# The last product of a linear-attention and MLP kernel, by seven block products in place of eight

## The chip, the cores and the metric

The kernel runs on one core of a Trainium2 chip. The metric is the device time of one execution in microseconds (us), the median of several runs. The engines named below are TensorE (PE, with its weight loads as PEld), VectorE (DVE), ScalarE (ACT) and SyncE (SP), whose queue issues all DMAs here.

## The reference, cut to what matters

```python
kv  = einsum('bhsd,bhse->bhde', k, v)          # 8 batches, 8 heads, 576 tokens, 64 dims
o   = einsum('bhsd,bhde->bhse', q, kv)
x   = o / sqrt(mean(o*o) + 1e-6) * g_norm      # rows of heads joined: 4608 tokens x 512
h   = x @ w_in                                 # 512 x 2048
x   = (h * clip(h + 3, 0, 6) / 6) @ w_out      # 2048 x 512
g   = x @ w_gate; val = x @ w_val              # 512 x 1536 each
out = (g * sigmoid(g) * val) @ w_out2          # 1536 x 512: the last product
```

All of it is fp32; the weights arrive as 64-bit floats and are decoded on the chip.

## The kernel before, in words

A product of two fp32 matrices is made of three matmuls of rounded operands: each operand is split into a high part (ScalarE copies it into a rounded type) and a low part (VectorE subtracts the high part from the source), by `split`, L105; `mm3`, L110, multiplies high by low, low by high and high by high into one accumulator.

The second MLP has two stages. The gate/value stage (`gv_step`, L682; `quad`, L657) runs over six blocks of 768 tokens, each visited twice (`visits`, L935): once for the first half of the gate/value weights, then, in reverse order, for the second half. A visit has three steps, a step two quads, one of gate and one of value. A quad makes a two by two block of the result by seven products of sums (`product`, L647, six matmuls of 384 columns each) in place of eight; the sums of weights come from `combine`, L490, which makes seven operand tiles from two decoded weight tiles, and `operands`, L479, which names them; the sums of x come from `prepare_x`, L608. The seven tiles of most pairs of the second half are stored in DRAM (`wsd`) in the first visits and loaded back when the visits turn round (`reload`, L940). The result of a step, `hv`, goes to DRAM as `g2d` (L687), feature blocks of 128 by all tokens. 36 steps in all, `c` from 0 to 35; the second half of the visits is c = 18 to 35.

The last product (L986 to L996) multiplies `g2d` by w_out2. It runs over nine blocks of 512 tokens, from the last to the first, and in each over the twelve feature blocks f. `load_g2`, L692, loads 512 tokens of one f (256 KB) and splits them; `o2_step`, L701, takes the four slices of 128 tokens as stationary operands and the 512 columns of w_out2 as moving ones: 4 x 3 matmuls of 512 columns, each with a weight load. Loads are issued eight f ahead. After f = 11 the four accumulators are copied out and stored (L711 to L718). w_out2 is decoded and split in steps 18 to 21 (f = 0 to 3) and 33 to 35 (the other eight), L979 to L981.

Space: the pool `w` (L86) has 58 slots of 256 KB. 42 of them hold gate/value sums through the second half of the visits; the rest are for what is on its way. The PSUM pool `ps` (L929) has four tags of one bank each, twice.

The order of the work: TensorE's instructions run in the order in which they are written (`manual_schedule`, L723). For the other engines and for the DMA queue a planner orders the instructions at build time, by the order of the text and by what it reckons to be ready. Each engine and SP's queue then go through that order one by one.

## Time and profile before

| | |
|---|---|
| median of 3 runs | 1720.38 us (1719.48 to 1722.3) |
| the profiled execution | 1719.0 us from its first to its last instruction; no other time of it is given |
| TensorE busy | 1688.9 us, 98% of the span |
| VectorE busy | 1185.0 us, 69% |
| ScalarE busy | 773.3 us, 45% |
| DMA | 252 MB, 147 GB/s on average |
| gate/value stage | about 890 to 1419.5 us of the span |
| last product | 1419.6 to 1715.2 us |

TensorE is almost always busy, so the table says little by itself; what a stage costs is the number of its matmuls and the distance between their starts, and where that distance breaks, a wait stands behind it. A matmul's recorded length overlaps the next one's, so lengths are not to be summed; starts are to be compared. The distances and waits are in the rows further down.

### The profile page before, as it was taken

The numbers are of one execution on the slowest core, as the hardware profiler recorded it, in microseconds if no ns is written. First come the engines' busy times: TensorE is split into PE (matmuls) and PEld (weight loads), VectorE is DVE, ScalarE is ACT, GpSimd is POOL, SyncE is SP. The second block draws the span as 40 slices with busy tenths as digits, with TensorE's granted clock in tenths as the row PEclk, the third lists the DMA queues.
The fourth block names the chain that finished last, engine by engine and source line by source line (L and its number), as shares of the span: only waits on it lengthen the run. The fifth ranks groups of instructions, "written<-read, shape, count | busy, mean of one in ns | idle before, by whom it ended". The sixth has DMA issues, their size and how long they took to land.

```text
span 1719.0 us, 25593 instructions
## 1 busy us (share of the span) xinstructions
PE 1688.9 (98%) x9636; PEld 1493.1 (87%) x9636; DVE 1185.0 (69%) x2353; ACT 773.3 (45%) x1439; POOL 2.4 (0%) x7
## 2 busy tenths in 40 slices
PE   7999999999999999999999999999999999999999
PEld 3566789898898899998889999999999997888887
DVE  5897987778777777777889888777666685322321
ACT  4565554445444454545555444434443453222221
POOL 0000000000000000000000000000000000000000
PEclk8999999999999999999999999999999999999999
DMA  7886444454545444325465544572222235334332
GB/s 191 248 259 188 130 138 128 146 149 115 160 127 159 126 148 131 123 99 184 151 205 178 198 147 149 184 260 76 81 91 92 92 135 182 125 111 143 140 110 74
DMA packets 200171, 252.29 MB, mean 147 GB/s; under 512 B 79984, under 2 KB 129136, under 8 KB 200048
## 3 DMA queue, kind: packets, MB, share of 16 engines
q1 hardware_dynamic: 200048, 250.67, 45.0%
q8 instruction: 75, 1.23, 0.3%
q14 instruction: 48, 0.39, 0.1%
HBM read 185.86 MB, written 64.75 MB: 146 GB/s over the span
## 4 chain that ended last, share of the span: by engine, by line
PE 86%; DVE 8%; ACT 2%; DMA 2%; issue 1%; SPq 0%; DVEq 0%; ACTq 0%
PE q_g L651 14%; PE q_v L651 14%; PE acc L111 12%; PE acc L112 12%; PE acc L113 12%; PE a L651 6%; PE d L651 4%; PE c L651 4%; PE h L117 3%; PE kv L250 1%; DMA raw_g<-in_moe_w_gate_dram 1%; DVE lT L108 1%; DVE g L108 1%; DVE t L580 1%; PE at L112 0%
## 5 line engine op out<-in xcount | busy, mean ns | idle before, releaser
L111 PE MATMUL acc<-g,wo 128*128 128x512 f32 x512 | 202.1, 395 | 0.0
L112 PE MATMUL acc<-g,wo 128*128 128x512 f32 x512 | 199.9, 390 | 0.0
L113 PE MATMUL acc<-g,wo 128*128 128x512 f32 x512 | 199.5, 390 | 0.0
L108 DVE TENSOR_TENSOR g2l<-g,g2h 128x512 fp32r<-128x512 f32 x108 | 73.4, 692 | 139.1 <-ACT g2h L107 138.5
L111 PE MATMUL acc<-wl,g2h 128*128 128x512 f32 x432 | 168.2, 389 | 1.0 <-ACT g2h L107 1.0
L112 PE MATMUL acc<-wh,g2l 128*128 128x512 f32 x432 | 168.2, 389 | 0.3 <-DVE g2l L108 0.3
L113 PE MATMUL acc<-wh,g2h 128*128 128x512 f32 x432 | 168.1, 389 | 0.0
L579 ACT ACTIVATE t<-h,three 128x512 f32<-128x512 f32 x120 | 86.7, 722 | 138.8 <-DVE h L574 109.5
L107 ACT ACTIVATE g2h<-g 128x512 fp32r<-128x512 f32 x108 | 67.9, 632 | 147.7 <-PE acc L112 74.3
L107 ACT ACTIVATE g<-t 128x512 fp32r<-128x512 f32 x144 | 90.9, 631 | 88.8 <-DVE t L580 73.6
L108 DVE TENSOR_TENSOR g<-t,g 128x512 fp32r<-128x512 f32 x144 | 97.9, 680 | 31.6 <-ACT g L107 31.2
L113 PEld LDWEIGHTS acc<-g,wo 128*128 128x128 f32 x512 | 96.1, 188 | 20.5
L111 PEld LDWEIGHTS acc<-g,wo 128*128 128x128 f32 x512 | 96.2, 188 | 19.9
L112 PEld LDWEIGHTS acc<-g,wo 128*128 128x128 f32 x512 | 96.2, 188 | 18.3
L111 PEld LDWEIGHTS acc<-wl,g2h 128*128 128x128 f32 x432 | 81.1, 188 | 18.0 <-ACT g2h L107 1.4
L112 PEld LDWEIGHTS acc<-wh,g2l 128*128 128x128 f32 x432 | 81.1, 188 | 17.5 <-DVE g2l L108 0.6
L580 DVE SCALAR_TENSOR_TENSOR t<-t,h 128x512 f32<-128x512 f32 x120 | 82.6, 688 | 19.3 <-ACT t L579 15.7
L113 PEld LDWEIGHTS acc<-wh,g2h 128*128 128x128 f32 x432 | 81.1, 188 | 16.9
L117 PE MATMUL h<-x,w_i 128*128 128x512 f32 x192 | 87.0, 602 | 1.9 <-DVE w_i L170 1.9
L117 PEld LDWEIGHTS h<-x,w_i 128*128 128x128 f32 x192 | 36.7, 193 | 43.2 <-issue 40.2
L651 PE MATMUL q_v<-hT,v 128*128 128x384 f32 x288 | 73.6, 336 | 0.0
L679 ACT ACTIVATE hg<-q_g 128x384 f32<-128x384 f32 x36 | 17.6, 490 | 113.3 <-PE q_g L651 113.3
(245 smaller groups left out, 4483.3 us busy)
## 6 DMA issues: line engine op xcount, KB each, us to landing
wo<-wod SPq DMA_DIRECT2D x128, 512.0 KB, 3.4
g2d<-hv SPq DMA_DIRECT2D x36, 768.0 KB, 3.4
g<-g2d SPq DMA_DIRECT2D x108, 256.0 KB, 4.6
xr<-x1d SPq DMA_DIRECT2D x11, 1536.0 KB, 6.7
x1d<-x1o SPq DMA_DIRECT2D x36, 256.0 KB, 2.9
out_dram<-o SPq DMA_DIRECT2D x36, 256.0 KB, 2.1
raw_i<-in_moe_w_in_dram SPq DMA_DIRECT2D x16, 512.0 KB, 5.3
raw_o<-in_moe_w_out_dram SPq DMA_DIRECT2D x16, 512.0 KB, 4.4
```

The source lines that it names most:

```text
L107: nc.scalar.activation(out=hi, in_=src, func=AF.Copy)
L108: nc.vector.tensor_tensor(out=lo, in0=src, in1=f32(hi), op=ALU.subtract)
L111: nc.tensor.matmul(out_, wh, xl, start=start, stop=False)
L112: nc.tensor.matmul(out_, wl, xh, start=False, stop=False)
L113: nc.tensor.matmul(out_, wh, xh, start=False, stop=stop)
L117: nc.tensor.matmul(out_, f32(w), f32(x), start=start, stop=stop)
L250: nc.tensor.matmul(ps[h * D:(h + 1) * D, :D], kt[:, h, r, :], vt[:, h, r, :], start=i == 0, stop=i == len(steps) - 1,)
L579: nc.scalar.activation(out=t, in_=h[i], func=AF.Relu, bias=three[:, 0:1])
L580: nc.vector.scalar_tensor_tensor(out=t, in0=t, scalar=6.0, in1=h[i], op0=ALU.min, op1=ALU.mult)
L651: nc.tensor.matmul(ps, a[:, kk], b[:, kk], start=first and n == 0, stop=n == 5, skip_group_check=True,)
L679: nc.scalar.activation(out=h[:, 0], in_=a, func=AF.Copy)
```

## The change

The last product takes the form that the gate/value stage has. A pair q of feature blocks (2q and 2q+1) and two halves of 256 tokens make a two by two block of g; w_out2's two feature blocks and its two halves of 256 columns make one of the weights. Seven products of sums replace eight, and each is a row of matmuls of 256 columns.

It runs in two phases per block of tokens: first, over all six pairs, the four products that need T1, T3, B11 and T2 (`o2_one`), then, over all six pairs, the three that need B22, T4 and B21 (`o2_two`). Between the two, u and v are formed from the accumulators, and phase two adds to three of them. The operands of g are made for two pairs at once (a unit): `g_one` loads four feature blocks (1 MB) into one tile and makes the sums and the high and low parts for phase one, `g_two` loads two feature blocks again and splits them and T4 for phase two. The first unit is made by `g_first` in slots of the pool `w`, since the new pools are not open then. Units are prepared two ahead.

The sums of w_out2 are made in steps 18 to 29, half a pair each (`make_w2`), are stored in DRAM (`w2d`, 42 tiles), and are loaded back by `reload_w2`: pairs 0 and 1 after the third and second last step, pairs 2 and 3 after the last, pairs 4 and 5 after the pools of the gate/value stage are closed.

```diff
+    TO2 = TO // 2
...
-    wraw = ctx.enter_context(tc.tile_pool(name="wraw", bufs=3))
+    mlp2 = ExitStack()
+    wraw = mlp2.enter_context(tc.tile_pool(name="wraw", bufs=3))
...
-    fpool = ctx.enter_context(tc.tile_pool(name="f", bufs=4, side="right"))
+    fpool = mlp2.enter_context(tc.tile_pool(name="f", bufs=4, side="right"))
...
+    w2d = dram.tile([NQ, 7, P, DM], F32, name="w2d")
...
@@ -689,33 +692,153 @@
             in_=hv.rearrange("p (f n) c -> p f (n c)", f=2),
         )
-    def load_g2(j, f):
-
-        raw = w_slot(f"g2_{j}_{f}", F32).rearrange("p k f -> p (k f)")
-        nc.sync.dma_start(out=raw, in_=g2d[f, :, j * TO:(j + 1) * TO])
-        hi = w_slot(f"g2h_{j}_{f}", F32R).rearrange("p k f -> p (k f)")
-        lo = w_slot(f"g2l_{j}_{f}", F32R).rearrange("p k f -> p (k f)")
-        split(hi, lo, raw)
-        return hi, lo
-
-    def o2_step(j, f, g, ps):
-        for i in range(TO // P):
+    def load_w2_pair(q, half):
+
+        raw = wraw.tile([P, KD, P, 2], U32, tag="raw", name=f"raw_2{q}_{half}")
+        nc.sync.dma_start(
+            out=raw.rearrange("p (f k) c t -> p f (k c t)", f=2),
+            in_=w_out2[2 * q * P:2 * (q + 1) * P, half * DM:(half + 1) * DM].rearrange(
+                "(f p) c -> p f c", p=P
+            ),
+        )
+        return decode_w(raw, f"2{q}_{half}")
+
+    def flat(o):
+        return o.rearrange("p k f -> p (k f)")
+
+    def w2_operands(q, tiles):
+        w2[q] = {
+            key: tuple(flat(o) for o in ops) for key, ops in operands(tiles).items()
+        }
+
+    def g2_rows(f0, n, r0):
+        return g2d[f0:f0 + n, :, r0:r0 + TO].rearrange("f p t -> p f t")
+
+    g_ops, t4s = {}, {}
+
+    def slot(name, dtype=F32):
+        return flat(w_slot(name, dtype))
+
+    def sub(out_, a, b):
+        nc.vector.tensor_tensor(out=out_, in0=a, in1=b, op=ALU.subtract)
+
+    def g_first(j, q):
+
+        n = f"{j}_{q}"
+        ra, rb, t13 = slot(f"ra_{n}"), slot(f"rb_{n}"), slot(f"t13_{n}")
+        for i, r in enumerate((ra, rb)):
+            nc.sync.dma_start(out=r, in_=g2d[2 * q + i, :, j * TO:(j + 1) * TO])
+        if q % 2 == 0:
+            t4s[j, q // 2] = slot(f"t4_{n}").rearrange("p (n c) -> p n c", n=2)
+        sub(t13[:, :TO2], ra[:, TO2:], ra[:, :TO2])
+        sub(t13[:, TO2:], rb[:, TO2:], ra[:, TO2:])
+        sub(ra[:, TO2:], rb[:, TO2:], t13[:, :TO2])
+        sub(t4s[j, q // 2][:, q % 2], ra[:, TO2:], rb[:, :TO2])
+        for keys, src in ((("T1", "T3"), t13), (("B11", "T2"), ra)):
+            hi, lo = slot(f"gh_{n}", F32R), slot(f"gl_{n}", F32R)
+            split(hi, lo, src)
+            for i, key in enumerate(keys):
+                g_ops[j, q, key] = tuple(o[:, i * TO2:(i + 1) * TO2] for o in (hi, lo))
+
+    def g_one(j, u):
+
+        n = f"{j}_{u}"
+        raw = big["gr"].tile([P, 2, 2, TO], F32, tag="raw", name=f"graw_{n}")
+        nc.sync.dma_start(
+            out=raw.rearrange("p q f t -> p (q f) t"), in_=g2_rows(4 * u, 4, j * TO)
+        )
+        t13 = big["gt"].tile([P, 2, 2, TO2], F32, tag="t13", name=f"gt13_{n}")
+        t4 = t4s[j, u] = slot(f"t4_{n}").rearrange("p (n c) -> p n c", n=2)
+        sub(
+            t13, raw[:, :, :, TO2:],
+            raw[:, :, 0].rearrange("p q (b t) -> p q b t", b=2),
+        )
+        b12 = raw[:, :, 0, TO2:]
+        sub(b12, raw[:, :, 1, TO2:], t13[:, :, 0])
+        sub(t4, b12, raw[:, :, 1, :TO2])
+        hi, lo = (
+            big["gx"].tile([P, 2, 4, TO2], F32R, tag=f"x{o}", name=f"gx{o}_{n}") for o in "hl"
+        )
+        split(hi[:, :, 0:2], lo[:, :, 0:2], t13)
+        split(
+            hi[:, :, 2:4].rearrange("p q b t -> p q (b t)"),
+            lo[:, :, 2:4].rearrange("p q b t -> p q (b t)"), raw[:, :, 0],
+        )
+        for i in range(2):
+            for k, key in enumerate(("T1", "T3", "B11", "T2")):
+                g_ops[j, 2 * u + i, key] = hi[:, i, k], lo[:, i, k]
+
+    def g_two(j, u):
+
+        n = f"{j}_{u}"
+        raws_ = [slot(f"gb_{n}_{i}") for i in range(2)]
+        for i, r in enumerate(raws_):
+            nc.sync.dma_start(out=r, in_=g2d[4 * u + 2 * i + 1, :, j * TO:(j + 1) * TO])
+        hi, lo = (
+            big["gy"].tile([P, 2, 3, TO2], F32R, tag=f"y{o}", name=f"gy{o}_{n}") for o in "hl"
+        )
+        split(hi[:, :, 2], lo[:, :, 2], t4s.pop((j, u)))
+        for i, r in enumerate(raws_):
+            split(
+                hi[:, i, 0:2].rearrange("p b t -> p (b t)"),
+                lo[:, i, 0:2].rearrange("p b t -> p (b t)"), r,
+            )
+        for i in range(2):
+            for k, key in enumerate(("B21", "B22", "T4")):
+                g_ops[j, 2 * u + i, key] = hi[:, i, k], lo[:, i, k]
+
+    def g_product(ps, g, w, first):
+
+        for i in range(TO2 // P):
             cs = slice(i * P, (i + 1) * P)
-            mm3(
-                ps[i], g[0][:, cs], g[1][:, cs],
-                w2[f][0].rearrange("p k f -> p (k f)"), w2[f][1].rearrange("p k f -> p (k f)"),
-                f == 0, f == NF2 - 1,
-            )
-        if f < NF2 - 1:
+            for n, (a, b) in enumerate(((g[0], w[1]), (g[1], w[0]), (g[0], w[0]))):
+                nc.tensor.matmul(
+                    ps[:, i * TO2:(i + 1) * TO2], a[:, cs], b,
+                    start=first and i == 0 and n == 0, stop=n == 2, skip_group_check=True,
+                )
+
+    acc2 = {}
+
+    def o2_one(j, q):
+
+        if q == 0:
+            for i, k in enumerate("aecd"):
+                acc2[k] = big["ps"].tile([P, 512], F32, tag=f"q{i}", name=f"o2{k}_{j}")
+        for k, b, a in (
+            ("c", "T1", "S1"), ("d", "T3", "S3"), ("a", "B11", "A11"), ("e", "T2", "S2"),
+        ):
+            g_product(acc2[k], g_ops.pop((j, q, b)), w2[q][a], q == 0)
+        if q < NQ - 1:
             return
-        for i in range(TO // P):
-            o = wpool.tile([P, DM], F32, tag="w", name="o")
-            r0 = j * TO + i * P
-            if i % 2:
-                nc.vector.tensor_copy(o, ps[i])
-            else:
-                nc.scalar.activation(out=o, in_=ps[i], func=AF.Copy)
-            nc.sync.dma_start(out=out[r0:r0 + P, :], in_=o)
+        acc2["u"], acc2["v"] = slot(f"u_{j}"), slot(f"v_{j}")
+        for o, p, r in (("v", "c", "d"), ("u", "a", "e")):
+            nc.scalar.activation(out=acc2[o], in_=acc2[p], func=AF.Copy)
+            nc.vector.tensor_tensor(out=acc2[o], in0=acc2[o], in1=acc2[r], op=ALU.add)
+
+    def put(j, o, dm, tok):
+        r0 = j * TO + tok * TO2
+        nc.sync.dma_start(
+            out=out[r0:r0 + TO2, dm * TO2:(dm + 1) * TO2].rearrange("(s p) c -> p s c", p=P),
+            in_=o.rearrange("p (s c) -> p s c", c=TO2),
+        )
+
+    def o2_two(j, q):
+
+        for k, b, a in (("c", "B22", "S4"), ("d", "T4", "A22"), ("a", "B21", "A12")):
+            g_product(acc2[k], g_ops.pop((j, q, b)), w2[q][a], False)
+        if q == 0:
+            o = slot("o")
+            nc.vector.tensor_tensor(out=o, in0=acc2["u"], in1=acc2["v"], op=ALU.add)
+            put(j, o, 1, 1)
+        if q < NQ - 1:
+            return
+        for k, dm, tok in (("c", 0, 1), ("d", 1, 0)):
+            o = slot("o")
+            nc.vector.tensor_tensor(out=o, in0=acc2["u"], in1=acc2[k], op=ALU.add)
+            put(j, o, dm, tok)
+        o = slot("o")
+        nc.scalar.activation(out=o, in_=acc2["a"], func=AF.Copy)
+        put(j, o, 0, 0)
     new_batch = {j: j for j in range(B)}
...
-        big["x2"] = ctx.enter_context(tc.tile_pool(name="x2", bufs=1, reuse_waits="tile"))
-        big["h"] = ctx.enter_context(tc.tile_pool(name="h", bufs=3, reuse_waits="tile"))
+        big["x2"] = mlp2.enter_context(tc.tile_pool(name="x2", bufs=1, reuse_waits="tile"))
+        big["h"] = mlp2.enter_context(tc.tile_pool(name="h", bufs=3, reuse_waits="tile"))
...
@@ -945,9 +1068,21 @@
             wgv[kind, p] = operands(tiles)
         ready.clear()
-        order2 = [(j, f) for j in reversed(range(NT // TO)) for f in range(NF2)]
-        G_AHEAD = 8
-        G_FIRST = 3
+        JO = list(reversed(range(NT // TO)))
+        W2_STEPS = 2 * NQ
+        w2_half = {}
+
+        def make_w2(q, half):
+            w2_half[half] = load_w2_pair(q, half)
+            if half:
+                return combine([w2_half.pop(0), w2_half.pop(1)], f"2{q}")
+
+        def reload_w2(q):
+            tiles = [w_slot(f"2{q}_{i}", F32R) for i in range(7)]
+            for i in (2, 3, 4, 5, 0, 1, 6):
+                nc.sync.dma_start(out=flat(f32(tiles[i])), in_=w2d[q, i])
+            w2_operands(q, tiles)
+
         for c, (n, j, p) in enumerate(steps):
             i = c % NH
             nxt = visits[n + 1][0] if n + 1 < len(visits) else j
...
@@ -975,25 +1110,45 @@
                             reload(m)
             else:
-                f = c - NB2 * NH
-                last = {15: (4, 5, 6), 16: (7, 8), 17: (9, 10, 11)}
-                for f in last.get(f, (f,) if f < 4 else ()):
-                    w2[f] = split_w(load_w2nd("2", f), f"2{f}")
-            if c == len(steps) - 2:
-                g2 = {m: load_g2(*order2[m]) for m in range(G_FIRST)}
-
-
-        for c in range(len(order2) + G_AHEAD):
-            if G_FIRST <= c < len(order2):
-                g2[c] = load_g2(*order2[c])
-            if c >= G_AHEAD:
-                j, f = order2[c - G_AHEAD]
-                if f == 0:
-                    acc2 = [
-                        big["ps"].tile([P, 512], F32, tag=f"q{i}", name=f"acc2_{j}_{i}")
-                        for i in range(TO // P)
-                    ]
-                o2_step(j, f, g2.pop(c - G_AHEAD), acc2)
+                m = c - NB2 * NH
+                if m < W2_STEPS:
+                    tiles = make_w2(m // 2, m % 2)
+                    if tiles:
+                        for k, t in enumerate(tiles):
+                            nc.sync.dma_start(out=w2d[m // 2, k], in_=flat(f32(t)))
+            m = c - len(steps)
+            if m == -3:
+                reload_w2(0)
+                g_first(JO[0], 0)
+            elif m == -2:
+                reload_w2(1)
+                g_first(JO[0], 1)
+            elif m == -1:
+                reload_w2(2)
+                reload_w2(3)
+
+        mlp2.close()
+        big["gr"], big["gt"], big["gx"], big["gy"] = (
+            ctx.enter_context(
+                tc.tile_pool(name=n, bufs=b, side=o, reuse_waits="tile")
+            ) for n, b, o in (
+                ("gr", 2, "right"), ("gt", 1, "right"), ("gx", 3, "left"), ("gy", 2, "left"),
+            )
+        )
+        units = [(j, h, u) for j in JO for h in range(2) for u in range(NQ // 2)]
+
+        def prepare_g(n):
+            if 0 < n < len(units):
+                j, h, u = units[n]
+                (g_two if h else g_one)(j, u)
+
+        prepare_g(1)
+        reload_w2(4)
+        reload_w2(5)
+        for n, (j, h, u) in enumerate(units):
+            prepare_g(n + 2)
+            for q in (2 * u, 2 * u + 1):
+                (o2_two if h else o2_one)(j, q)
 # ---- launch: one core; inputs and outputs as the reference has them ----
```

## Rows read from the trace of the kernel before

**Rows 1.** The page's busy table and the slices of TensorE's granted clock.

```profile
PE 1688.9 (98%) x9636; PEld 1493.1 (87%) x9636; DVE 1185.0 (69%) x2353; ACT 773.3 (45%) x1439; POOL 2.4 (0%) x7
...
PEclk8999999999999999999999999999999999999999
```

**Rows 2.** Windows: the last product's stretch; columns are start:end, length, busy us per engine, clock, DMA.

```profile
1419.56:1715.20 295.64, 294.38 (x1297) 242.98 (x1296) 90.92 (x134) 80.04 (x129) 0.00 (x0) 1.00 0.36 125
```

**Rows 3.** Timeline, TensorE, start of the last product: start us, us, instruction, idle before.

```profile
1419.56 0.39 PE L111 MATMUL acc<-wl,g2h 128*128 128x512 f32 x1
...
1428.88 0.50 PE L111 MATMUL acc<-wl,g2h 128*128 128x512 f32 x1 [0.95 <-ACT g2h L107]
...
1429.68 0.50 PE L112 MATMUL acc<-wh,g2l 128*128 128x512 f32 x1 [0.31 <-DVE g2l L108]
...
1430.02 0.39 PE L113 MATMUL acc<-wh,g2h 128*128 128x512 f32 x1
```

**Rows 4.** Timeline of all engines, end of the span.

```profile
1713.98 2.47 SPq L718 DMA_DIRECT2D out_dram<-o  x4
...
1714.97 0.39 PE L113 MATMUL acc<-wh,g2h 128*128 128x512 f32 x1
...
1715.39 0.69 DVE L715 COPY o<-acc 128x512 f32<-128x512 f32 x1 [0.67 <-PE acc L113]
```

**Rows 5.** Timeline, TensorE, one pair of the first MLP and the line after it.

```profile
509.67 0.28 PE L651 MATMUL a<-lB,wh_i 128*128 128x256 f32 x1
...
514.71 0.40 PE L111 MATMUL acc<-g,wo 128*128 128x512 f32 x1
```

**Rows 6.** Windows, the same pair.

```profile
509.67:514.71 5.04, 5.04 (x43) 5.04 (x42) 3.79 (x8) 4.11 (x10) 0.00 (x0) 1.00 0.31 107
```

**Rows 7.** Lines by form, gate/value stage, VectorE and ScalarE: busy us, mean ns.

```profile
L686 DVE TENSOR_TENSOR hv<-hg,hv 128x1536 f32<-128x1536 f32 x15 | 26.3, 1752 | 1.0 <-ACT hv L679 1.0
...
L108 DVE TENSOR_TENSOR lB<-xr,hB 128x768 fp32r<-128x768 f32 x16 | 15.2, 952 | 0.0
...
L107 ACT ACTIVATE hB<-xr 128x768 fp32r<-128x768 f32 x15 | 12.6, 839 | 0.0
```

**Rows 8.** Lines by form, last product.

```profile
L108 DVE TENSOR_TENSOR g2l<-g,g2h 128x512 fp32r<-128x512 f32 x105 | 71.3, 692 | 136.8 <-ACT g2h L107 136.2
...
L107 ACT ACTIVATE g2h<-g 128x512 fp32r<-128x512 f32 x105 | 66.0, 632 | 142.5 <-PE acc L112 74.3 <-DMA g<-g2d 65.7 <-DVE g2l L108 0.7
...
L715 DVE COPY o<-acc 128x512 f32<-128x512 f32 x18 | 12.4, 692 | 66.6 <-PE acc L113 66.6
...
L717 ACT ACTIVATE o<-acc 128x512 f32<-128x512 f32 x18 | 10.8, 598 | 67.8 <-PE acc L113 67.8
```

**Rows 9.** Windows, a stretch of reloads of 256 KB beside the gate/value stage.

```profile
1133.00:1148.00 15.00, 15.00 (x88) 15.00 (x87) 8.20 (x14) 5.17 (x10) 0.00 (x0) 1.00 0.93 334
```

**Rows 10.** Windows, three visits of the gate/value stage.

```profile
940.41:985.14 44.73, 44.60 (x253) 43.87 (x253) 42.10 (x78) 22.98 (x42) 0.00 (x0) 1.00 0.57 206
...
985.14:1029.39 44.25, 44.25 (x253) 43.97 (x253) 36.56 (x67) 21.25 (x38) 0.00 (x0) 1.00 0.43 155
...
1206.12:1250.35 44.23, 44.23 (x253) 43.95 (x253) 30.84 (x54) 18.25 (x32) 0.00 (x0) 1.00 0.24 90
```

**Rows 11.** Chain of waits, one quad: start us, us.

```profile
1279.69 7.33 PE q_v L651 x42
```

**Rows 12.** Timeline, SP's queue: start us, us for all.

```profile
1131.02 5.32 SPq L944 DMA_DIRECT2D g<-wsd  x7
```

**Rows 13.** Waits: us in total, times, longest.

```profile
DVE g2l L108 <- ACT g2h L107: 138.5, 70, 4.9
```

More of the change, by code (lines that the diff above doesn't have):

```diff
@@ L917 @@
                         big["xr"], raw2, big["x"] = (
-                            ctx.enter_context(tc.tile_pool(name=o, bufs=1, side="right"))
+                            mlp2.enter_context(tc.tile_pool(name=o, bufs=1, side="right"))
                             for o in ("xr", "raw2", "x1")
```

## The prediction, made before the changed kernel was run

> **What bounds the kernel now.** First the page's busy table: TensorE is busy 98% of the span, at full clock from the second slice on [rows 1]. So time goes only where TensorE issues less, or issues faster; work on the other engines counts only if it makes TensorE wait. Next the stage that the change rewrites, the last product. Its stretch is 295.64 us [rows 2]. The timeline gives the pace there: the 1296 matmuls of 512 columns run from 1419.56 to the last start at 1714.97; from the 39th (1430.02) to the 1296th these are 1257 steps in 284.95 us, 0.2267 us each [rows 3, 4]. 1296 of them are 293.8 us; the other 1.8 us are a wait at the start, in front of the 37th and 38th matmul, for operands that ScalarE and VectorE made late [rows 3]. Beside them VectorE is busy 90.92 us and ScalarE 80.04 us of 295.64, and DMA moves 125 GB/s [rows 2]: three resources with room. After the last matmul stand one copy of 0.69 us and the last transfer, up to the end of the span [rows 4].
>
> **The change, part by part.**
>
> *The product itself.* Before: 9 blocks x 12 f x 4 x 3 = 1296 matmuls of 512 columns. After: 9 blocks x 6 pairs x 7 products x 2 token slices x 3 = 2268 matmuls of 256 columns, 7/8 of the columns. The kernel already runs this shape: each pair of the first MLP has 42 matmuls of 256 columns with a new weight load each, and they take 5.04 us from first start to the next line's first start [rows 5], 0.1200 us each; all 42 loads lie under them [rows 6]. 2268 x 0.1200 = 272.2 us. Against 295.6 us (the old start wait goes too) that is -23.4 us.
> The Trainium skill, "TensorE: Matmul & The Clock Gate", section "Back-to-back issue gap", lists 262 cycles for 256 columns and 518 for 512 at 2.4 GHz, so 109 and 216 ns; by it the stage would go from 279.7 to 247.6 us, a gain of 32 us. The rows give 120 and 227 ns for these two widths in this kernel, some 11 ns more per matmul, which costs more where there are more matmuls; the rows decide.
>
> *Preparing g.* Per block VectorE and ScalarE now make seven operands instead of one set. A one-unit (two pairs): the T1/T3 subtraction and two low parts of 1024 elements each, two subtractions of 512. An element of VectorE costs (1752 - 952) / 768 = 1.04 ns [rows 7], so 1024 elements take 952 + 256 x 1.04 = 1.22 us, and 512 take 0.69 [rows 8]: 3 x 1.22 + 2 x 0.69 = 5.04 us. A two-unit: three low parts of 512, 2.08 us. Evictions: five adds of 512, 3.5 us (before: two copies [rows 8]). Per block 3 x 5.04 + 3 x 2.08 + 3.5 = 24.8 us against 252 x 0.1200 = 30.2 us of TensorE: 82% full. ScalarE: 1024 elements are about 839 + 256 x 0.81 = 1.05 us (slope from 512 at 632 and 768 at 839 ns [rows 7, 8]); 3 x (2 x 1.05 + 3 x 0.63) + 3 x 0.60 = 13.8 us, 46%. DMA: g read 1.5 times (4.7 MB) and 1.05 MB out per block, 5.8 MB in 30.2 us = 190 GB/s against 334 shown for reloads [rows 9]. All of it lies beside TensorE, since preparation runs two units (5.8 and 4.3 us of matmuls) ahead with three buffers for one-units and two for two-units. Cost 0; if that cover fails it is the slower rival below.
>
> *Seams.* Each block has two, 18 in all: phase two accumulates into c, d and a, which must first be copied out. At the end of phase one c is ready 18 steps (2.2 us) before it is wanted, and ScalarE needs 0.63 us behind at most one instruction of 1.05; d is wanted 0.72 us after the phase's end and ready 1.44 before it, VectorE needs 0.69 behind at most 1.22: 0.25 us to spare; a has 0.5 to spare. So nothing if one preparation stands in front, a few tenths if two do. Behind the waiting matmul stands the whole queue of TensorE. The nearest row is what a change of token block costs in the stage before: a visit of 44.25 us holds six quads of 7.33 us [rows 10, 11], 0.27 us over. Bounds 0 and 18 x 0.27 = 4.9; I take 1.5, nearer to the sum of the margins.
>
> *The sums of w_out2.* Six pairs are decoded and combined in steps 18 to 29 of the gate/value stage, where before w_out2 was decoded and split (four f there, eight in the last three steps); this load disappears. VectorE is busy 30.84 us in a visit without weight work and 36.56 us in one with two decodes and one combination [rows 10]: 5.7 us per pair. Four visits get 1.5 pairs on average, the worst two combinations with three decodes: at most 30.84 + 11.4 = 42.3 of 44.25 us. A visit that full exists: 42.10 us busy, 44.73 long [rows 10], so 0.48 us lost. Bounds 0 and 4 x 0.48 = 1.9; I take 1.0. The added 42 stores and 42 reloads of 256 KB queue on SP with the stores of hv; seven reloads took SP 5.32 us to issue [rows 12], 42 take 32 us, spread over some 230 us. Cost 0, since a buffer of hv has a whole step (14.7 us) to be stored.
>
> *The start of the last product.* The w slots decide: 58, of which 42 hold gate/value weights until the end and come free seven at a time, after each quad of the last visit. Pairs 0 and 1 can come two steps before the end, 2 and 3 from the last step on, 4 seven us before the end, 5 at the end. TensorE wants pairs 4 and 5 two units (11.5 us) after the stage's start. From the last step's beginning to there are 26.2 us for four pairs (7.3 MB), one raw unit (1.05 MB) and an hv store (0.8 MB): 9.2 MB, at 334 GB/s [rows 9] 27.5 us. That is 1.3 us late, or not at all where pair 2 starts on slots freed earlier. Behind a reload that waits for its slot stand the next raw loads in SP's queue, so unit 2 is what comes late next. If nothing of this load starts before 7.3 us ahead of the end, it lands 8.7 us late. Bounds 0 and 8.7; I take 1.0.
>
> *The end.* Three results (two adds, one copy) and stores of 256 KB; the last is a copy of 0.60 us instead of 0.69 [rows 4, 8], with shorter rows in the store. Bounds -0.1 and +0.7 (one more result behind the last), I take 0.
>
> **Sum.** -23.4 + 1.5 + 1.0 + 1.0 = -19.9 us on the profiled execution's 1719.0 us span: 1699.1 us. No time of that execution other than its span is given; the median of the runs, 1720.38, is 1.4 us over it. Forecast: 1700.5 us. With all unknown costs at their ends: 1697.0 (none) to 1712.5 (all); its own range, 1697 to 1707.
>
> **The rivals.**
> 1. *Half of the gain goes in waits that TensorE did not have.* Several of the covers fail in part: late reloads (8.7), seams at their bound (4.9) or low parts that come a little late in each of the 27 one-units (0.3 us each is 8). For it: VectorE 82% full in the last stage and 95% in two visits. Against it: the visit with VectorE at 42.10 of 44.73 us lost only 0.48. Gain 6 to 15 us: 1706 to 1714.
> 2. *Slower: VectorE's queue becomes the bound of the last product.* One mechanism: in the order on VectorE each low part stands right behind its subtraction and waits for ScalarE's high part. Before, VectorE waited 138.5 us in 70 waits, 2 us each, for just that [rows 13], without harm because it had room. If each low part waited out its high part (1.05 us for 1024 elements, 0.63 for 512), a block would need 24.8 + 6 x 1.05 + 9 x 0.63 = 36.8 us of VectorE against 30.2 of TensorE: 9 x 6.6 = 59 us, or 40 us slower than before, 1760. It decides from 32.4 us per block on (30.2 plus the 2.2 us gained per block). Against it: two other instructions of 0.69 us stand between the first subtraction and its low part, and the next unit's work can fill the rest.
> 3. *The change does not shorten the stage at all:* the smaller share of columns is eaten by waits of 20 us, at the start above all (reloads of all six pairs only after the gate/value stage: 11 MB and 3 MB of g at 334 GB/s land 42 us after its end, pairs 4 and 5 being wanted at 11.5, so 30 us). For it: 42 of 58 slots are held until then. Against it: they come free by sevens, and SP has only this to do. 1717 to 1730.
> 4. *Weight loads come to light.* Each matmul of the new shape has its own 128-column load, 2268 instead of 1296; where a load isn't hidden, the pace is the load's recorded 188 ns, 2268 x 0.188 = 426 us, and the time 1850. The 42 matmuls at 0.1200 us with 42 loads under them [rows 5, 6] speak against it. The Trainium skill, same page, "The mechanism" in the part on packing small matmuls, says that weight loads overlap matmuls in flight only where the row group differs; by it this rival would hold, and the trace does not agree, at 120 ns per pair of load and matmul (it agrees with the same page's specification table, which has TensorE pull loads ahead of matmuls in flight).
>
> **How the numbers follow.** Forecast 0.66; rival 1 0.17; rival 2 0.08; rival 3 0.06; rival 4 0.01; better than 1697 (old waits elsewhere go too) 0.02. 0.2% (3.4 us) is about what a measurement of this kernel can tell from no change, so faster means below 1716.9: the forecast, rival 1 and the last, 0.85; within, half of rival 3 and a little of 2: 0.04; slower 0.11. The range takes in the unknown costs and most of rival 1: 1696 to 1712.
>
> **What would show it.** In the changed trace: a stage of 2268 matmuls with starts 0.120 us apart, 272 us plus few us; VectorE near 65 to 75% busy there; waits of TensorE under 2 us in the first 30 us of the stage, for reloaded w or for unit 2's operands; at the seams waits of d for VectorE of a few tenths; visits of 44.2 to 44.8 us with VectorE around 39 to 42. Wrong would be a pace above 0.125 us, a wait in each one-unit for VectorE's low parts, or a gap of over 5 us in front of the third unit.

## The result, and the profile after

The changed kernel takes 1704.95 us (median of four runs, 1703.2 to 1707.97) against 1720.96 us for the kernel before on the same chip (four runs): ratio 0.991, 95% interval 0.9897 to 0.9924, so 16 us faster. The forecast was 1700.5 us, 20 us faster; the time lies inside the range, 4.5 us over the forecast. The profiled execution took 1705.95 us, its span is 1704.2 us.

The page's busy table, to be read beside [rows 1]:

```profile
PE 1668.5 (98%) x10608; PEld 1522.4 (89%) x10608; DVE 1321.0 (78%) x2531; ACT 813.8 (48%) x1489; POOL 2.4 (0%) x7
```

TensorE is still the bound at 98%, with 972 more matmuls (2268 for 1296). The windows of the kernel after (start:end, length, busy us and count of PE, PEld, DVE, ACT, POOL, granted clock, DMA share, GB/s): two visits of the gate/value stage, the whole last product, its first 15.66 us, the 5 us within them in which DMA was fullest, and one block without a wait.

```profile
1207.82:1252.09 44.27, 44.27 (x254) 43.99 (x253) 39.88 (x74) 22.84 (x41) 0.00 (x0) 1.00 0.48 173
1252.09:1296.33 44.24, 44.24 (x253) 43.96 (x253) 40.16 (x74) 22.76 (x41) 0.00 (x0) 1.00 0.49 179
...
1421.34:1699.89 278.55, 273.85 (x2269) 272.44 (x2268) 203.15 (x254) 111.58 (x160) 0.00 (x0) 1.00 0.55 185
...
1421.34:1437.00 15.66, 15.66 (x132) 15.66 (x132) 10.49 (x11) 5.64 (x8) 0.00 (x0) 1.00 0.92 326
1432.00:1437.00 5.00, 5.00 (x44) 5.00 (x43) 0.63 (x1) 0.04 (x1) 0.00 (x0) 1.00 1.05 393
...
1484.00:1514.24 30.24, 30.24 (x252) 30.09 (x252) 24.03 (x30) 13.42 (x20) 0.00 (x0) 1.00 0.57 192
```

The last row is the forecast's pace: 252 matmuls in 30.24 us, 0.1200 us each, with 252 loads under them. The stage is 278.55 us, against 295.64 in [rows 2]: 272.2 us at that pace and 6.3 us of waits. TensorE's timeline has them all in one kind of place, the seam from phase one to phase two of a block (start, us, instruction; in brackets the idle time before it and what ended it). The rows below are the stage's first start, the largest of these waits, and the last start:

```profile
1421.34 0.28 PE L795 MATMUL o2c<-20_3_15137,gh 128*128 128x256 f32 x1
...
1440.80 0.38 PE L795 MATMUL o2c<-20_5_15139,gyh 128*128 128x256 f32 x1 [2.04 <-ACT v L815]
...
1442.51 0.39 PE L795 MATMUL o2d<-20_6_15140,gyh 128*128 128x256 f32 x1 [0.74 <-DVE v L816]
...
1624.82 0.39 PE L795 MATMUL o2c<-20_5_15139,gyh 128*128 128x256 f32 x1 [0.84 <-ACT v L815]
...
1626.38 0.39 PE L795 MATMUL o2d<-20_6_15140,gyh 128*128 128x256 f32 x1 [0.59 <-DVE v L816]
...
1657.32 0.39 PE L795 MATMUL o2d<-20_6_15140,gyh 128*128 128x256 f32 x1 [0.45 <-DVE v L816]
...
1699.77 0.28 PE L795 MATMUL o2a<-25_0_15505,gyh 128*128 128x256 f32 x1
```

At the first seam ScalarE's copy of c (`v<-o2c`) is late. Its timeline, in the same form, says why:

```profile
1436.96 1.33 ACT L109 ACTIVATE gyh<-gb 128x512 fp32r<-128x512 f32 x2 [7.43 <-DMA gb<-g2d]
1438.19 1.04 ACT L109 ACTIVATE gxh<-gt 128x1024 fp32r<-128x1024 f32 x1
1439.13 1.13 ACT L109 ACTIVATE gyh<-gb 128x512 fp32r<-128x512 f32 x2
1440.17 0.58 ACT L815 ACTIVATE v<-o2c 128x512 f32<-128x512 f32 x1
```

ScalarE stood 7.43 us at a preparation whose load had not landed, and then had four more preparations to do before the copy. VectorE, which adds d to that copy, stood behind its own late load (first row), with further preparations between:

```profile
1436.37 1.22 DVE L723 TENSOR_TENSOR gt<-graw 128x1024 f32<-128x1024 f32 x1 [4.45 <-DMA graw<-g2d]
...
1440.57 1.28 DVE L110 TENSOR_TENSOR gyl<-gb,gyh 128x512 fp32r<-128x512 f32 x2
1441.78 0.68 DVE L816 TENSOR_TENSOR v<-v,o2d 128x512 f32<-128x512 f32 x1
```

And SP's queue shows why the loads were late. Into it were written, in this order, the last store of hv, the seven reloads of pair 5, the next block's raw g and four loads of g for phase two (start, us for all, count):

```profile
1423.84 0.37 SPq L690 DMA_DIRECT2D g2d<-hv  x1
1424.31 0.42 SPq L1083 DMA_DIRECT2D 25_2_15507<-w2d  x1
...
1428.40 0.44 SPq L747 DMA_DIRECT2D graw<-g2d  x1
1428.93 2.35 SPq L776 DMA_DIRECT2D gb<-g2d  x4
```

The loads of g were issued 7.6 us after the stage's start, behind 1.8 MB of reloads, and DMA ran at 393 GB/s while they were under way (second last window row above). Issued at 1428.93, the first was in use at 1436.96, 8.0 us later.

At the later seams, in all of blocks 2 to 8, the two queues have one order: ScalarE copies c behind the two high parts of a one-unit of the next block, the first of which waits for VectorE's subtraction, and VectorE adds d behind that unit's two low parts. Where nothing is lost, as in the sixth block, the order is the same and the copy only came earlier. In the seventh block the subtraction had itself waited for its load (VectorE, then ScalarE):

```profile
1620.95 1.23 DVE L723 TENSOR_TENSOR gt<-graw 128x1024 f32<-128x1024 f32 x1 [1.63 <-DMA graw<-g2d]
...
1624.51 1.22 DVE L110 TENSOR_TENSOR gxl<-graw,gxh 128x1024 fp32r<-128x1024 f32 x1
1625.64 0.68 DVE L816 TENSOR_TENSOR v<-v,o2d 128x512 f32<-128x512 f32 x1
```

```profile
1622.27 1.06 ACT L109 ACTIVATE gxh<-gt 128x1024 fp32r<-128x1024 f32 x1 [4.56 <-DVE gt L723]
...
1624.18 0.58 ACT L815 ACTIVATE v<-o2c 128x512 f32<-128x512 f32 x1
```

Where the 14.8 us between the two profiled spans (1719.0 and 1704.2) come from: the last product -17.1 (295.64 to 278.55); the gate/value stage from its first steady quad on +0.1 (902.73 to 1419.56 before, 904.43 to 1421.34 after: 516.83 and 516.91); everything ahead of that quad, where the two kernels issue the same instructions in the same order on every engine, +1.7; the end after the last matmul +0.5 (3.8 us in [rows 4], 4.3 now). The 1.7 us isn't the change: over the eleven profiles of the experiments below, all with the same code up to there, this quad starts between 901.61 and 904.99.

### The profile page after: what moved, and what is told of

Its sections match the earlier page's. It is cut to its first block, busy times and chain, and to the rows that moved or that the text cites. A ratio compares the mean times of both kernels' runs of the same rounds, so it can differ in the third digit from the quotient of the medians.

```text
span 1704.2 us, 27886 instructions
## 1 busy us (share of the span) xinstructions
PE 1668.5 (98%) x10608; PEld 1522.4 (89%) x10608; DVE 1321.0 (78%) x2531; ACT 813.8 (48%) x1489; POOL 2.4 (0%) x7
## 4 chain that ended last, share of the span: by engine, by line
PE 81%; DVE 10%; DMA 4%; ACT 3%; issue 2%; SPq 1%; DVEq 0%; ACTq 0%
PE q_g L654 15%; PE q_v L654 14%; PE acc L113 7%; PE acc L114 7%; PE acc L115 7%; PE a L654 6%; PE d L654 4%; PE c L654 4%; PE h L119 3%; PE o2d L795 3%; PE o2a L795 3%; PE o2c L795 3%; PE o2e L795 1%; DMA gb<-g2d 1%; PE kv L253 1%
## 5 line engine op out<-in xcount | busy, mean ns | idle before, releaser
L110 DVE TENSOR_TENSOR lT<-T,hT 128x384 fp32r<-128x384 f32 (+1 forms) x120 | 68.0, 588 | 0.8 <-ACT hT L109 0.2
L654 PE MATMUL a<-lB,wh_i 128*128 128x256 f32 x240 | 68.1, 284 | 0.0
L654 PE MATMUL a<-hB,wh_i 128*128 128x256 f32 x240 | 67.9, 283 | 0.0
L654 PE MATMUL a<-hB,wl_i 128*128 128x256 f32 x240 | 67.9, 283 | 0.0
L572 DVE TENSOR_TENSOR v<-v,d 128x256 f32<-128x256 f32 x60 | 25.1, 419 | 54.3 <-PE d L654 54.1
L689 DVE TENSOR_TENSOR hv<-hg,hv 128x1536 f32<-128x1536 f32 x36 | 63.1, 1754 | 5.1 <-ACT hv L682 4.9
L109 ACT ACTIVATE hT<-T 128x384 fp32r<-128x384 f32 (+1 forms) x120 | 60.5, 548 | 2.7 <-DVE T L625 2.5
L682 ACT ACTIVATE hv<-q_v 128x384 f32<-128x384 f32 x36 | 17.8, 494 | 87.2 <-PE q_v L654 87.2
```

The source lines that it names most:

```text
L109: nc.scalar.activation(out=hi, in_=src, func=AF.Copy)
L110: nc.vector.tensor_tensor(out=lo, in0=src, in1=f32(hi), op=ALU.subtract)
L654: nc.tensor.matmul(ps, a[:, kk], b[:, kk], start=first and n == 0, stop=n == 5, skip_group_check=True,)
L682: nc.scalar.activation(out=h[:, 0], in_=a, func=AF.Copy)
L689: nc.vector.tensor_tensor(out=hv, in0=hg, in1=hv, op=ALU.mult)
```

## The experiments

Theory A: the 4.5 us over the forecast are the waits at the seams, and these come from what stands ahead of the copies of c and d in the two in-order engines. The rivals: B, VectorE is close to its limit over the whole stage and the waits show that; C, the pace itself suffers from the preparation beside it. All kernels below are the changed kernel with the edit shown. "Stage" is the last product in the run's profile; "waits" is the stage less 272.3 us. The last two columns say where: how much TensorE's steps from start to start are longer than 0.12 us, in sum, around the first seam and around the later ones; what is left of the waits lies elsewhere (to within 0.2 us). A wait costs about 0.25 us more than the idle time in its row, since the step that it ends and the one behind it are longer too. r9 to r11 ran on another chip than r1 to r8; each ratio is to the kernel before on the same chip.

| run | median us | ratio to before (95%) | stage us | waits us | first seam | later seams |
|---|---|---|---|---|---|---|
| the change | 1704.95 | 0.9910 (0.9897 to 0.9924) | 278.55 | 6.3 | 3.3 | 3.1 |
| r1_again | 1704.86 | 0.9907 (0.9891 to 0.9924) | 277.37 | 5.1 | 2.7 | 2.6 |
| r2_by_product | 1698.28 | 0.9871 (0.9856 to 0.9885) | 274.48 | 2.2 | 0.1 | 2.1 |
| r3_fresh_banks | 1698.23 | 0.9866 (0.9851 to 0.988) | 272.32 | 0.0 | 0 | 0 |
| r4_no_last_reloads | 1699.87 | 0.9876 (0.9862 to 0.9891) | 273.99 | 1.7 | 0 | 1.9 |
| r5_sums_kept | 1698.48 | 0.9872 (0.9855 to 0.989) | 273.61 | 1.3 | 0 | 0 |
| r6_one_repeat | 1704.30 | 0.9905 (0.989 to 0.9921) | 276.73 | 4.4 | 0 | 0 |
| r7_three_repeats | 1734.48 | 1.0085 (1.0069 to 1.0101) | 308.28 | 36.0 | 0 | 0 |
| r8_prepared_once | 1697.85 | 0.9874 (0.9856 to 0.9891) | 272.14 | 0 | 0 | 0 |
| r9_both | 1698.22 | 0.9867 (0.9852 to 0.9882) | 272.92 | 0.6 | 0.3 | 0 |
| r10_evict_first | 1713.47 | 0.9960 (0.9945 to 0.9975) | 285.44 | 13.1 | 1.8 | 11.5 |
| r11_store_later | 1702.51 | 0.9895 (0.9878 to 0.9911) | 276.32 | 4.0 | 1.6 | 2.2 |

**r1_again.** No edit.

> The changed kernel once more, to part what recurs from what varies. First theory (evictions at the seam stand behind preparations in the queues of ScalarE and VectorE): TensorE waits again 5 to 7 us in the last product, all at seams between phase one and two, 3 us of it in the first block; the stage is again about 278 us long. The gate/value stage starts between 902.5 and 905 us, since nothing before it is ordered otherwise than before: the 1.7 us later start of the first profile is variation. Rival (the early part is slower by the change): it starts near 904.4 again. Median 1703 to 1706.

Its first seam has 1.40 us idle before c and 0.74 before d; the later ones have three waits of 0.4 to 0.6, all before d. The seams wait in each run of the kernel; which of the later ones do varies.

**r2_by_product.** The two pairs of a unit are taken inside each product, so that the last matmul on c and on d lies 36 steps ahead of the next use in place of 18. The work is the same.

```
-            for q in (2 * u, 2 * u + 1):
-                (o2_two if h else o2_one)(j, q)
+            (o2_two if h else o2_one)(j, (2 * u, 2 * u + 1))
...
-            g_product(acc2[k], g_ops.pop((j, q, b)), w2[q][a], q == 0)
+            for r in qs:
+                g_product(acc2[k], g_ops.pop((j, r, b)), w2[r][a], r == 0)
```

> In each unit the loop over products is outside and the two pairs inside, so c is ready 36 steps (4.3 us) ahead of the seam instead of 18, and d and a get twice their time too. First theory (evictions late in their queues by up to 3 us): the waits at later seams (1.75 and 0.6 us) go, the first block's 3.1 us fall to 1 or so; sum of TensorE's waits in the last product from 6.2 to under 2 us, the median 4 to 5 us lower, about 1700.5. Rival (VectorE has too little room in the last product, 73% busy with bursts): the waits stay 5 us or more in sum, at the seams or in front of units, and the time stays at 1705.

The first seam has no wait any more; one wait of the size seen before is left, in the seventh block. Windows of the stage and the timeline row of that wait:

```profile
1421.56:1696.04 274.48, 273.87 (x2269) 272.58 (x2268) 202.89 (x254) 111.00 (x160) 0.00 (x0) 1.00 0.56 189
```

```profile
1622.37 0.39 PE L795 MATMUL o2c<-20_5_15139,gyh 128*128 128x256 f32 x1 [0.53 <-ACT v L817]
```

VectorE is as busy as before (202.89 for 203.15), so B doesn't explain the waits. The median is 6.6 us below r1_again's, more than the 4 to 5 expected; the profiled execution is the slowest of this kernel's four (1701.89 us), and its stage is 2.9 us shorter than r1_again's. The shares came out the other way round: I expected the later seams' waits to go and 1 us of the first seam's to stay; the first seam's went whole, and of the later ones' 2.6 us 2.1 stayed.

**r3_fresh_banks.** Phase two accumulates into three other PSUM buffers and doesn't wait for the copies. Phase one's share of three of the four results is left out.

```
+        if q == 0:
+            for i, k in ((0, "a"), (2, "c"), (3, "d")):
+                acc2[k] = big["ps"].tile([P, 512], F32, tag=f"q{i}", name=f"o2{k}2_{j}")
-            g_product(acc2[k], g_ops.pop((j, q, b)), w2[q][a], False)
+            g_product(acc2[k], g_ops.pop((j, q, b)), w2[q][a], q == 0)
```

> Phase two accumulates into the other buffers of c, d and a, so it waits for no eviction; what phase one left in c, d and a is not added to the outputs. First theory: no wait at any seam, the last product is 272.2 us and at most 1 us more, the time 6 us lower, 1699. Rival (VectorE has too little room): the preparation of units is late instead, and at least 3 of the 6 us of waits come back in front of units of phase two or one.

```profile
1420.06:1692.38 272.32, 272.32 (x2269) 272.14 (x2268) 202.44 (x254) 110.31 (x160) 0.00 (x0) 1.00 0.56 189
```

Without the dependence the stage runs without a gap: 2268 matmuls at 0.1200 us. So the waits are the seams' and nothing else's, the forecast's pace holds over the whole stage, and late reloads and late operands together cost no more than 0.2 us here.

**r4_no_last_reloads.** Pairs 4 and 5 use the weights' sums of pairs 0 and 1; 14 of 42 reloads are left out, and so the last of the queue ahead of the loads of g.

```
-        reload_w2(4)
-        reload_w2(5)
+        w2[4], w2[5] = w2[0], w2[1]
```

> The sums of pairs 4 and 5 are not loaded back; the products use those of pairs 0 and 1 in their place, so 14 loads of 256 KB (3.7 MB) at the start of the last product are left out, and the work is otherwise the same. First theory with the start's cause (the first block's loads of g for phase two stand in SP's queue and in the DMA engines behind the reloads and land at 15 us into the stage): the first seam's wait falls from 3.1 to under 0.5 us, the later seams stay as they fall (0 to 3 us), time 1701 to 1703. Rival (VectorE has too little room): the first seam keeps 2 us or more.

The first seam's wait is gone: ScalarE stands 2.51 us at its load instead of 7.43, the load being in use 5.5 us after its issue (at 1423.81) in place of 8.0, and the copy waits for TensorE, not TensorE for the copy (timeline of ScalarE):

```profile
1429.26 1.31 ACT L109 ACTIVATE gyh<-gb 128x512 fp32r<-128x512 f32 x2 [2.51 <-DMA gb<-g2d]
...
1433.87 0.60 ACT L815 ACTIVATE v<-o2c 128x512 f32<-128x512 f32 x1 [1.31 <-PE o2c L795]
```

Small waits at later seams stay (1.9 us by the table). The median is below the 1701 to 1703 expected. So the first seam's part comes from the reloads ahead of the loads of g at the start, and the later ones' doesn't. The edit also leaves 14 slots of the pool `w` free for other tiles; this run alone doesn't part that from the missing traffic.

**r8_prepared_once.** The operands of g are made for the first block and used for all nine, so the loads and preparations of eight blocks are left out (VectorE 43.30 us busy in place of 203). The third unit of phase two uses the first one's operands, so two of the six loads of g for phase two are missing in the first block too.

```
-                g_ops[j, 2 * u + i, key] = hi[:, i, k], lo[:, i, k]
+                g_ops[2 * u + i, key] = hi[:, i, k], lo[:, i, k]
...
+                if j != JO[0]:
+                    return
```

> The operands of g are made for the first block only and used for all nine (the third unit of phase two uses the first one's), so loads and preparation of g are left out from the second block on. First theory: the seams of blocks two to nine cost nothing, the first seam keeps its 2.5 to 3 us (less what the next block's loads added to it), the last product is 272.3 + 1 to 3 us, 1698 to 1702. Rival (the pace of 0.120 us itself suffers from preparing beside it): the pace falls under 0.120 us and the stage under 272 us.

```profile
1419.66:1691.80 272.14, 272.14 (x2269) 272.10 (x2268) 43.30 (x59) 23.53 (x37) 0.00 (x0) 1.00 0.14 49
```

The waits I expected at the first seam are missing. The reloads of pairs 4 and 5 are all there; what is missing ahead of the first seam is the next block's raw load with its preparation, and the two loads just named. ScalarE's load is in use 5.5 us after its issue (at 1426.74), as in r4:

```profile
1432.27 1.97 ACT L109 ACTIVATE gyh<-gb 128x512 fp32r<-128x512 f32 x3 [4.42 <-DMA gb<-g2d]
```

So the reloads alone are not enough: it needs the other loads and preparations too, and which of these is not shown. And 2268 matmuls with hardly anything beside them take what they take with VectorE at 74% (272.32 in r3): that refutes C.

**r11_store_later.** The last store of hv is written behind the reload of pair 5, so that the reloads don't stand in SP's queue waiting for it.

```
+        if c < 2 * NB2 * NH - 1:
+            store()
+        else:
+            late.append(store)
...
         reload_w2(5)
+        late.pop()()
```

> The store of the last hv is written after the reload of pair 5, so that the reload doesn't stand behind it in SP's queue. Theory on the first seam (loads of g land late since SP stands some 4 us at that store with the reload and the loads behind it): loads of g issue 2 to 4 us earlier, the first seam's wait falls from 2.5 to 3.1 us to under 1, time 1702. Rival (the DMA engines are full there, whatever SP does): it keeps 1.5 us or more.

The loads for phase two are issued 5.35 us after the stage's start, not 7.59; the first seam has 1.15 us idle, all before d, in place of 2.14 (r1_again) and 2.78. It goes about half of the way, between the two expectations, and the later seams are not touched: 2.2 us are theirs. TensorE's wait, and ScalarE's for the first load:

```profile
1439.14 0.39 PE L804 MATMUL o2d<-20_6_15140,gyh 128*128 128x256 f32 x1 [1.15 <-DVE v L825]
```

```profile
1432.97 1.28 ACT L109 ACTIVATE gyh<-gb 128x512 fp32r<-128x512 f32 x2 [5.52 <-DMA gb<-g2d]
```

These loads are issued as early as in r4 (5.24 us there), yet the first is in use 8.4 us after its issue (at 1424.61) and not 5.5. So the time in SP's queue makes one part of the first seam's wait; the other goes with the traffic around the loads, to which the reloads (missing in r4) and the next block's raw load (missing in r8) both belong.

**r10_evict_first.** The preparation of unit n + 2 is written behind the product of a phase's last unit, so that the copies stand ahead of it in the queues.

```
-            prepare_g(n + 2)
+            if u < NQ // 2 - 1:
+                prepare_g(n + 2)
...
+            if u == NQ // 2 - 1:
+                prepare_g(n + 2)
```

> The preparation two units ahead is written after the last unit's product of each phase and not before it, so the evictions of that unit come earlier in the text. First theory: in ScalarE's order at the first seam one pair of instructions less stands between the late load and v (3 in place of 5); the first seam costs 1 to 2 us in place of 2.5 to 3.1, later seams 0 to 1.5 in sum, 1702 to 1703. Rival (the waits come from the loads' lateness alone, whatever stands behind it): the first seam keeps its 2.5 us.

This missed: 8.6 us slower than r1_again, not faster. The first seam fell to 0.68 us idle before c and 0.58 before d, but now nearly every seam has a wait, on c as on d (waits of TensorE in the stage: total us, times, longest):

```profile
PE o2c L795 <- ACT v L815: 5.4, 7, 1.5
PE o2d L795 <- DVE v L816: 3.7, 8, 0.6
```

VectorE now waits 28.3 us in 15 waits for raw g, after 13.3 in 9 (waits of VectorE in the stage, the change and then r10):

```profile
DVE gt L723 <- DMA graw<-g2d: 13.3, 9, 4.5
...
DVE gt L723 <- DMA graw<-g2d: 28.3, 15, 4.1
```

These loads are issued a unit later, and what they hold up runs into the next seam: from the fourth block to the eighth ScalarE's copy of c stands behind high parts of two one-units, where in the change it is one, and the last of them comes after a wait of 2.7 us. In the fourth block:

```profile
1533.06 1.06 ACT L109 ACTIVATE gxh<-gt 128x1024 fp32r<-128x1024 f32 x1 [2.67 <-DVE gt L723]
1534.02 0.58 ACT L815 ACTIVATE v<-o2c 128x512 f32<-128x512 f32 x1
```

**r5_sums_kept and r9_both.** Versions that compute everything. r5: r3's other buffers, with c and a copied out, u added to c and d at the seam, and the parts added at the end (three more adds per block on VectorE). r9: r5 and r2 together.

```
+        for o in ("u", "v", "sa", "sc", "sd"):
+            acc2[o] = slot(f"{o}_{j}")
...
+        add("sd", "u", "d")
+        add("sc", "u", "sc")
...
-            nc.vector.tensor_tensor(out=o, in0=acc2["u"], in1=acc2[k], op=ALU.add)
+            nc.vector.tensor_tensor(out=o, in0=acc2["s" + k], in1=acc2[k], op=ALU.add)
```

> Phase two accumulates into the other buffers of c, d and a, and what phase one left is added to the outputs: c and a are copied out at the seam, u is added to c and d there, and three adds at the end of phase two make the outputs. All of the result is computed, with three more VectorE instructions of 512 elements per block (8 for 5 and a copy of ScalarE less). First theory (the cost was the evictions' order at the seam): no wait at the seams, the last product 272.3 to 273 us, time 1698 to 1700, some 6 us under the changed kernel. Rival (VectorE has too little room): the 2.1 us more of VectorE per block bring back waits of 3 us or more in sum.

> Products outside and pairs inside, as in the run by product, and fresh banks with the sums kept; the whole result is computed. First theory: neither the seams nor the 1.4 us in front of the fifth unit remain, since the eviction of c now stands ahead of the loads' instructions in ScalarE's order; the last product 272.2 to 273 us, 1697 to 1698. Rival (VectorE at 80% of each block has too little room): 2 us of waits or more, 1699 to 1701.

In neither does TensorE stand idle at a seam; r5 has one wait of 1.19 us in the first block, for a low part of g. r2, r5 and r9 agree within 0.3 us: about 22.5 us faster than before and 6.5 faster than the change. The stages of the profiles differ by less: 278.0 us on average in the two of the change, 273.7 in these three. These 4.3 us are located; the other 2 us of the medians are not, since runs without a profile show no place.

**r6_one_repeat and r7_three_repeats.** How much room VectorE has: r3 (with what it leaves out) and the second low part of each one-unit computed twice, or four times.

```
+        nc.vector.tensor_tensor(
+            out=lo[:, :, 2:4].rearrange("p q b t -> p q (b t)"), in0=raw[:, :, 0],
+            in1=f32(hi[:, :, 2:4]).rearrange("p q b t -> p q (b t)"), op=ALU.subtract,
+        )
```

> As the run with fresh banks (phase one's part of c, d and a left out of the outputs), with each one-unit's second low part computed twice: 1.13 to 1.22 us of VectorE more per unit, 3.5 us per block, so some 26.3 of 30.24 us busy (87%). First theory (VectorE has room, order was the cost): the last product stays at 272.3 to 273 us, 1698. Rival (VectorE is the bound or nearly): 9 x 3.5 = 31 us more, or at least 5.

> As before, with the second low part computed four times: 10.3 us of VectorE more per block, 22.8 + 10.3 = 33.1 us against 30.24 of TensorE. Both theories: VectorE is now the bound, 8 blocks x 2.9 = 23 us more at least, 1720; in front of units TensorE waits for low parts. It shows where the slower rival of the prediction begins: past 30.2 us of VectorE per block.

Windows of r6, the stage and one block without a wait, and a wait of TensorE:

```profile
1421.42:1698.15 276.73, 273.48 (x2269) 272.39 (x2267) 230.01 (x280) 112.14 (x160) 0.00 (x0) 1.00 0.55 186
...
1511.00:1541.24 30.24, 30.24 (x254) 30.24 (x253) 26.27 (x32) 12.61 (x18) 0.00 (x0) 1.00 0.52 170
```

```profile
1632.60 0.39 PE L799 MATMUL o2c<-24_4_15496,gyl 128*128 128x256 f32 x1 [1.22 <-DVE gyl L110]
```

r6 fell between what the theories expected. Over the stage VectorE is 83% busy (230.01 of 276.73), 87% in that block, which lost nothing. Five of the nine blocks lose next to nothing; in the others four waits of up to 1.2 us, all for a low part of g, make the stage 4.4 us longer than r3's. r9 has VectorE busy 217.05 of 272.92 us, 80%, and loses 0.6. The two runs add their work at different places, so how full VectorE is may not be all that parts them.

Windows of r7, the stage and five stretches of 1 us behind a wait, and the wait:

```profile
1421.96:1730.24 308.28, 286.77 (x2269) 284.90 (x2267) 284.71 (x332) 116.58 (x160) 0.00 (x0) 0.95 0.49 167
...
1540.50:1541.50 1.00, 0.87 (x4) 0.87 (x5) 1.00 (x3) 0.11 (x1) 0.00 (x0) 0.58 0.00 0
1541.50:1542.50 1.00, 1.00 (x6) 1.00 (x6) 1.00 (x3) 0.00 (x0) 0.00 (x0) 0.50 0.63 86
1542.50:1543.50 1.00, 1.00 (x6) 1.00 (x6) 1.00 (x1) 0.00 (x0) 0.00 (x0) 0.50 0.87 315
1543.50:1544.50 1.00, 1.00 (x8) 1.00 (x7) 0.02 (x1) 0.03 (x1) 0.00 (x0) 0.71 1.06 414
1544.50:1545.50 1.00, 1.00 (x11) 1.00 (x10) 0.24 (x1) 1.00 (x2) 0.00 (x0) 1.00 1.03 399
```

```profile
1540.63 0.58 PE L800 MATMUL o2a<-24_0_15494,gxl 128*128 128x256 f32 x1 [2.31 <-DVE gxl L768]
```

VectorE is 284.71 us busy, 31.6 per block for 30.24 of TensorE. The stage is 36.0 us longer than r3's, of which VectorE's work above TensorE's 272.3 explains 12.4. By TensorE's own row, 21.5 us are idle (308.28 - 286.77) and 14.5 are longer steps (286.77 - 272.32). VectorE isn't busy all the time either: at the seams it stands and waits for d (waits of VectorE in the stage), with preparations behind it in its queue, so the two engines hold each other up in turn:

```profile
DVE v L821 <- PE o2d L800: 14.0, 9, 2.7
```

## Why the prediction came out as it did

**The product: right.** 0.1200 us per matmul was forecast from one pair of the first MLP and measured over a whole stage (272.32 us in r3 for 272.2). The gap figure of the Trainium skill, "TensorE: Matmul & The Clock Gate", section "Back-to-back issue gap", which the page gives for a matmul in isolation (262 cycles, 109 ns, for 256 columns), would have given an estimate of 247.6 us; the measurement decides against it. Rival 4, weight loads in the open, is refuted: 2268 loads lie under 2268 matmuls.

**Preparing g beside TensorE: right, with little to spare.** The two terms that were worked out by slope came out at 1.221 us on VectorE and 1.054 on ScalarE for 1024 elements. A block takes 24.0 us of VectorE in its window (24.8 forecast), the stage 73% (65 to 75). Rival 2 named 32.4 us per block as the point from which VectorE decides. In r7, at 31.6, the kernel is slower than before already, so that point lies lower, between r6's 25.6 (230.01 over nine blocks) and 31.6; r6 pays 4.4 us. The change itself stands at 22.6 (203.15 over nine blocks) and its own waits for operands of g are nil. The waits that rival 2 named are there, 41.1 us in 20 waits of VectorE for ScalarE's high parts, and cost TensorE nothing.

**The sums of w_out2: hidden, nearly free.** The gate/value stage took +0.1 us, forecast +1.0, bounds 0 to 1.9. The two visits above are 44.27 and 44.24 us long with VectorE at 39.88 and 40.16.

**The start of the last product: no wait, forecast +1.0.** Unit 2's operands and weights came in time: the first 15.66 us have no gap. But the DMA crowd that I priced there was real. It fell on the next wait downstream, the first seam, because the loads of g for phase two queue behind the reloads.

**The seams: the term that was too small.** Forecast 1.5 us, bounds 0 to 4.9; measured 6.3 and 5.1 us in the two profiles of the change. The mechanism was named (c, d and a must be copied out while phase two waits); the step that failed is "behind at most one instruction": at the first seam five preparations stood ahead of the copy of c, the first of them waiting 7.43 us for a DMA; at the later seams two stand ahead of the copy and two ahead of the add of d, the first of them waiting for VectorE. I had counted the length of the instruction in front, not what that instruction itself waits for. For two in front the prediction had "a few tenths", and the later seams show it: 0.4 to 0.6 us idle before d where they wait. The sign "waits of TensorE under 2 us in the first 30 us" failed at the first seam: 2.78 us, for the copies and not for reloaded w or unit 2's operands.

r3 takes the dependence away and all waits at the seams go. r2 adds slack: the first seam's go, of the later seams' 2.6 to 3.1 us 2.1 stay. r4, r8 and r11 show that the first seam needs the reloads together with the loads and preparations behind them. The later seams' waits go in r3, r5, r8 and r9, where phase two has its own buffers or there is nothing to prepare. Why VectorE reaches the subtraction later in one block than in another of the same order stays open.

**The sum.** Of the 4.5 us over the forecast: seams +4.8, start -1.0, sums of w_out2 -0.9, end +0.5; with 1.7 us by which the unchanged part of this profile ran later it makes 5.1, on the span (1704.2 for 1699.1). Of rival 1 (several covers fail in part) one part came true, the seams, a little past their bound of 4.9; the late reloads and late low parts did not. That the sum missed by no more than this is in part luck: the start and the sums of w_out2, which came out at nothing or near it, took back 1.9 us of what the seams added.

## What to carry to other kernels

Where an accumulator is handed over between two uses, the slack has to cover everything that stands ahead of the copy in its engine's queue, and each instruction there with its own longest wait, DMAs included. A second buffer (r5, r9) took the waits at all seams away; more steps between the last use and the next one (another loop order, r2) took the first seam's and left 2.1 us at the later ones. Each gave back some 6.5 us in the median. Writing the copy earlier relative to the preparations moved the waits and made them larger (r10). VectorE, hidden behind TensorE, cost nothing at 74% of the stage (r3), 0.6 us at 80% (r9) and 4.4 us at 83% (r6).

## What the hardware showed that I had not expected

A wait of TensorE can cost more than its length. In r7, behind 2.31 us of idle time at 1540.63, the granted clock is 0.50, the lower of its two levels (1.2 GHz), for some 3 us and then 1.00 again: 6 matmuls fall into a stretch of 1 us, 11 at full clock. This is in the rows above. Eight of r7's nine waits are followed by such a stretch; one, as long as seven of them, is not (second block; timeline of TensorE, then a window):

```profile
1473.55 0.38 PE L800 MATMUL o2a<-24_0_15494,gxl 128*128 128x256 f32 x1 [2.30 <-DVE gxl L768]
```

```profile
1475.30:1476.30 1.00, 1.00 (x11) 1.00 (x10) 1.00 (x1) 0.42 (x1) 0.00 (x0) 1.00 0.86 293
```

That block loses 2.55 us, each of the seven after it 3.9 to 4.1. Over the stage (mean clock 0.95) the low clock makes some 12 us: the 36.0 less 21.5 of idle time and less 0.25 for each wait, which it costs at full clock too. In the change itself TensorE idled 2.04 us before 1440.80 and went on at full clock (a step of 0.22 us right behind it, then of 0.12), and the stage's mean is 1.00. So the length of a wait alone doesn't tell whether the clock falls, and no run here shows what does.
